# Two of a turn's 32 exponential blocks made on VectorE in the second attention

## The chip, the cores and the metric

The kernel runs on one core of a Trainium2 chip, as one program. The metric is device time in microseconds (us). Before the change it took 2643.88 us, the median of three runs (2642.66 to 2646.45). A core's engines work through instruction streams of their own and wait for each other on semaphores: TensorE (PE, matrix products into PSUM; PEld is its weight loading), ScalarE (ACT), VectorE (DVE), GpSimd (POOL) and SyncE (SP), the last two mainly issuing transfers here.

## The reference

Four layers with residuals: attention, a state-space convolution, the same attention again, the same convolution again. The change concerns the third layer, which is computed as the first one.

```python
def _A_ref(x, wqkv, wo):                     # x: 1 x 2048 x 640, 32 heads of 20
    qkv = (x @ wqkv) ... q, k, v             # by head
    scores = einsum("bhqd,bhkd->bhqk", q, k) * (Dh ** -0.5)
    p = softmax(scores, axis=-1)
    o = einsum("bhqk,bhkd->bhqd", p, v)
    return o.transpose(0, 2, 1, 3).reshape(B, S, D) @ wo

x = x + _A_ref(layernorm(x), A_wqkv, A_wo)
x = x + _B_ref(layernorm(x), ...)            # state-space convolution
x = x + _A_ref(layernorm(x), A_wqkv, A_wo)   # the second attention
x = x + _B_ref(layernorm(x), ...)
```

## The kernel before, in words

An attention goes in 32 **turns**. A turn is four heads (a group `g` of eight) and 512 of the 2048 queries. It walks over 16 tiles of 128 keys (`kt`), and for each over two pairs of heads (`j`), so it has 32 **score blocks** of 128 x 1024. For each block `scores` (L868) issues eight small products on TensorE, which fill different parts of the array together, into the PSUM tile `S`, and one exponential on ScalarE, `pt<-S`, into SBUF. There are two `S` tiles (four PSUM banks) and seven `pt` tiles (`PB`). After the two blocks of a key tile, `values` (L903) multiplies both `pt` with the values `V` into the two accumulators `pa` (one bank each, and one pair for all turns). `V` has a column of ones, so the sums of the softmax come with it. At the end of a turn VectorE copies and adds the two `pa` into `oc`; the sums of the rows go through DRAM and back by GpSimd transfers (`dn`, `dr`, `db`), VectorE inverts them, and `oc` is scaled and stored (`ot`).

Beside this TensorE has other work, in the two remaining PSUM banks `m0` and `m1`: the projections of later heads (`jobs`: `qk`, L620, 15 steps into both banks, then five VectorE operations on 128 x 512 that empty them and split the result into `qhi` and `qlo`; `vq`, L586, values of a later group; `norms`, L548), and in the last eight turns the first part of the output projection (`rows_out`, L1078, weights `woh` and `wol`, rows `oh` and `ol`). The last eight turns take the last two groups alternately.

**What sets the order.** Instructions of an engine start in the order of its program. While the program is written, a `Plan` keeps a rough clock of TensorE, ScalarE and VectorE, and it decides where things are put. After each score block `fill` runs: it issues a value product when its exponentials will be ready, then `slot` puts in steps of the projections that end before ScalarE needs a next score (`until`), and `drain_later` and `weave` put in work of VectorE whose time has come. `slot` without a limit puts the next step in whatever it delays. `chain` ties TensorE's products in the order written, and the other engines are tied likewise in an attention. Line 78 of the profile is the wrapper through which ScalarE, VectorE, GpSimd and SyncE operations are recorded.

Of the kernel before, what the change touches and what calls it, by code (L numbers as in the profile page):

```python
# [21 lines left out]
P = 128  # L22
# [20 lines left out]
MAGIC = 1.5 * 2.0 ** 23  # L43
TWO_PI = 6.283185
# [6 lines left out]
class Plan:  # L51


    def __init__(self):
        self.pe = self.act = self.dve = 0.0
        self.keep, self.fixed = False, 0.07
# [6 lines left out]
class Ordered:  # L63
# [5 lines left out]
    def __getattr__(self, name):  # L69
# [4 lines left out]
        def call(out, *a, **k):  # L74
            if self.count:
                big = a[0].shape if "reduce" in name else out.shape
                self.plan.dve = max(self.plan.dve, self.plan.pe - 0.9) + self.plan.fixed + math.prod(big[1:]) / 960
            made = f(out, *a, **k)  # L78
# [9 lines left out]
def mha_s4d_kernel(ctx, tc, x_in, wqkv, wo, lar, aim, cr, ci, ldt, dsk,  # L88
# [319 lines left out]
    pend, slow = [], []  # L408
    free = [0.0, 0.0]
# [22 lines left out]
    def attention(x, stats):  # L432
# [282 lines left out]
        def slot(until=None):  # L715
# [3 lines left out]
            begun = head[0] and head[0][2]  # L719
            if pend and part[0] is None and not begun and (head[0] is None or spent[0] >= ahead(len(ends) - 2)):  # L720
# [134 lines left out]
        plan.keep, plan.fixed = True, 0.11 if first_layer else 0.07  # L855
# [3 lines left out]
        ready, scaled, stored = [], [], {}  # L859

        def scores(kt_, kc, qt):
# [3 lines left out]
            for t in range(4):  # L865
                for r in range(2):
                    rows = slice(64 * r, 64 * r + NK)
                    chain(te.matmul(S[32 * t:32 * t + 32, 512 * r:512 * r + 512],  # L868
                                    kt_[rows, kc + 32 * t:kc + 32 * t + 32], qt[rows, :],
                                    start=True, stop=True, tile_position=(64 * r, 32 * t)))  # L870
# [24 lines left out]
        def values(qb, g, kt, pts, pa):  # L895

            V = Vt[g // 2 % 3]
            plan.on_pe(0.865)
            for r in range(2):
                rows = slice(64 * r, 64 * r + 64)  # L900
                for j in range(4):
# [3 lines left out]
                                    start=(kt == 0), stop=(kt == NI - 1), tile_position=(64 * r, 32 * j)))  # L905
            if kt == NI - 1:
# [47 lines left out]

        def end_jobs():
# [17 lines left out]
            if not first_layer:  # L973
                xpools.pop().__exit__(None, None, None)
# [18 lines left out]
        class Rows:  # L993

            def __init__(self, w2, n):
                self.w2, self.n, self.loaded = w2, n, []
                self.mv = w2.tile([P, NI, 2], F32, bufs=1, name="mvx")
                self.whole = set()
# [24 lines left out]
        def normalise(rows, x, s):  # L1023
# [18 lines left out]
            def parts():  # L1042
                u = rows.w2.tile([P, D], F32, bufs=1, name="u")
                ve.tensor_scalar(u, x[:, s, :], mv[:, 0:1], y, ALU.subtract, ALU.mult)
                ve.tensor_copy(uh[:, s, :], u)
                later.append((plan.dve + 0.5, lambda: ve.tensor_sub(ul[:, s, :], u, uh[:, s, :])))
# [47 lines left out]
        last[0] = None  # L1094
        tail, rows, stop = None, None, []
# [5 lines left out]
        for n, (g, qb) in enumerate(turns):  # L1101
# [15 lines left out]
            g2, qb2 = turns[n + 1] if n + 1 < len(turns) else (g, 0)  # L1117
            for kt in range(NI):
                kc, pts = P * (kt % 8), []
                for j in range(2):  # L1120
                    pts.append(scores(kop[j][kt // 8], kc, qop[j][n % 2]))
                    if j:
                        ready.append((plan.act, qb, g, kt, pts, pa))
                    fill(j)
# [6 lines left out]
                if kt == 12 and first_layer and n == len(turns) - 1:  # L1131
                    late.append(ve.last)
                if kt == 8 and g2 != g:
# [6 lines left out]
        for r_ in ready:  # L1140
            values(*r_[1:])
# [652 lines left out]
```

## Time and profile before

| what | us |
|---|---|
| runs: median (lowest to highest) | 2643.88 (2642.66 to 2646.45) |
| the profiled execution, first to last instruction (its span; no other time of it is given) | 2647.0 |
| second attention's score blocks, first exponential to the last | 1469 to 2451 |
| a turn there, 982 us over 32 | 30.7 |
| ScalarE busy in these 982 us | 967 |
| VectorE busy in these 982 us | 296 |

A busy TensorE in the table of the profile is not TensorE at its peak, since its ends are modelled and its products overlap. Start times in a timeline are the better measure of what it holds.

### The profile page before, as it was taken

To read this page: it belongs to the slowest core of one execution; us is meant where nothing else is said; L and a number is where in the kernel's file an instruction comes from. 1 tells how busy PE (TensorE), PEld (TensorE's weight loads), DVE (VectorE), ACT (ScalarE), POOL (GpSimd) and SP (SyncE) were. 2 spreads that over 40 slices of the span, in tenths; PEclk is the share of its full clock that TensorE was granted. 3 is DMA by queue.
4 is the path that set the end of the run, shared out by engine and by line. 5 is a ranking of instruction groups with operands and counts; after the bars stand their busy time and mean duration, and the time that the engine had idled before them with its cause. 6 is when DMAs were issued, how large, how long until landed. Compare 5 with 4: busy or idle time off the path is not lost.

```text
span 2647.0 us, 118800 instructions
## 1 busy us (share of the span) xinstructions
PE 2492.4 (94%) x52388; PEld 1409.8 (53%) x52388; DVE 1519.5 (57%) x3430; ACT 2344.0 (89%) x2763; POOL 801.7 (30%) x1230
## 2 busy tenths in 40 slices
PE   6899999999999999899898999999999998999898
PEld 3444444454444444587896544454444443444898
DVE  7587777777765887577786323232232222143875
ACT  7899999999999999655665899999999999999574
POOL 1123333233323332111681122222222223222285
PEclk9999999999999999999999999999999999999999
DMA  6522222322222221654652111121121113222466
GB/s 206 189 53 77 68 74 62 82 65 63 61 54 59 53 63 38 234 206 163 213 173 64 47 53 50 51 60 45 45 66 39 50 34 87 71 66 61 137 190 184
DMA packets 188158, 241.99 MB, mean 91 GB/s; under 512 B 43504, under 2 KB 128816, under 8 KB 186224
## 3 DMA queue, kind: packets, MB, share of 16 engines
q1 hardware_dynamic: 151936, 188.28, 22.6%
q0 software_dynamic: 35696, 46.01, 7.4%
q8 instruction: 413, 6.77, 1.1%
q14 instruction: 113, 0.93, 0.1%
HBM read 158.16 MB, written 76.00 MB: 88 GB/s over the span
## 4 chain that ended last, share of the span: by engine, by line
ACT 59%; PE 20%; issue 10%; DVE 3%; DMA 2%; POOL 1%; SPq 0%; ACTq 0%; POOLq 0%; DVEq 0%
ACT pt L78 57%; PE psy L1430 3%; PE pa L903 2%; PE psv L1430 2%; PE po L193 2%; PE psx L1430 2%; PE S L868 2%; PE pst L1452 1%; PE pkx L193 1%; PE pv L586 1%; PE m L620 1%; PE pkt L196 1%; PE pq L773 1%; DMA kb<-khb 1%; DMA kop<-ks 1%
## 5 line engine op out<-in xcount | busy, mean ns | idle before, releaser
L78 ACT ACTIVATE pt<-S 128x1024 f32<-128x1024 f32 x2048 | 1927.7, 1033 | 27.9 <-PE S L868 15.5
L903 PE MATMUL pa<-pt,V 64*32 64x512 f32 x16384 | 1096.9, 589 | 1.4 <-DVE oc L78 1.4
L868 PE MATMUL S<-qop,kop 61*32 61x512 f16 x16384 | 877.2, 380 | 82.7 <-ACT pt L78 67.8
L868 PEld LDWEIGHTS <-kop 61*32 61x32 f16 x16384 | 366.9, 89 | 737.3 <-issue 619.2
L903 PEld LDWEIGHTS pa<-pt,V 64*32 64x32 f32 x16384 | 312.7, 106 | 72.0 <-issue 8.6
L78 POOL DMA_DIRECT2D dn<-oc x248 | 122.7, 501 | 574.2 <-DVE oc L78 574.1
L78 DVE TENSOR_SCALAR qc<-m 128x512 f32<-128x512 f32 (+1 forms) x68 | 46.8, 688 | 312.0 <-PE m L620 312.0
L78 POOL DMA_DIRECT2D db<-dn x248 | 125.4, 512 | 141.5 <-DMA dn<-dr 136.9
L78 POOL DMA_DIRECT2D ot<-oc x256 | 130.5, 517 | 88.4 <-DVE oc L78 55.5
L620 PE MATMUL m<-xl,wh 64*32 64x512 f16 x2560 | 143.8, 376 | 0.3 <-issue 0.3
L620 PE MATMUL m<-xh,wh 64*32 64x512 f16 x2560 | 144.1, 378 | 0.0
L620 PE MATMUL m<-xh,wl 64*32 64x512 f16 x2560 | 143.8, 377 | 0.0
L78 DVE COPY oc<-pa 128x512 f32<-128x512 f32 x64 | 44.2, 690 | 172.9 <-PE pa L903 168.9
L78 ACT COPY xt<-pst 128x1024 f16<-128x1024 f16 x80 | 81.3, 1016 | 60.8 <-PE pst L1452 60.8
L620 PEld LDWEIGHTS <-wh 64*32 64x32 f16 x5120 | 90.3, 93 | 73.3 <-issue 30.8
L78 POOL DMA_DIRECT2D dn<-dr x62 | 34.6, 558 | 287.3 <-DVE dr L78 248.6
L1480 POOL TENSOR_TENSOR kb<-t,kb 128x512 f32<-128x512 f32 x76 | 97.2, 1280 | 65.2 <-DVE t L78 40.8
L78 DVE TENSOR_SCALAR V<-m 128x160 f32<-128x160 f32 x64 | 20.7, 324 | 163.4 <-PE m L586 163.4
L78 DVE TENSOR_TENSOR kb<-ktab 128x512 f32<-128x512 f32 x160 | 106.2, 683 | 0.0
L586 PEld LDWEIGHTS <-xh 128*128 128x128 f16 x960 | 79.7, 98 | 46.7 <-issue 31.4
L1480 POOL TENSOR_TENSOR ka<-ka,kb 128x512 f32<-128x512 f32 x76 | 97.5, 1283 | 6.0
L337 PEld LDWEIGHTS m<-kb,ka 128*32 128x32 f32 x3840 | 60.8, 109 | 71.0 <-issue 52.4
(312 smaller groups left out, 3936.4 us busy)
## 6 DMA issues: line engine op xcount, KB each, us to landing
ka<-kha SPq DMA_DIRECT2D x80, 256.0 KB
kb<-khb SPq DMA_DIRECT2D x80, 256.0 KB
db<-dn POOLq DMA_DIRECT2D x248, 64.0 KB, 3.2
kop<-ks SPq DMA_DIRECT2D x176, 80.0 KB
kpw<-wd POOLq DMA_DIRECT2D x60, 192.0 KB, 3.9
qop<-qs SPq DMA_DIRECT2D x256, 40.0 KB
ot<-oc POOLq DMA_DIRECT2D x256, 40.0 KB, 3.0
kha<-kn SPq DMA_DIRECT2D x20, 512.0 KB
```

The costliest lines, as they stand in the source:

```text
L78: made = f(out, *a, **k)
L193: chain(te.matmul(*a, **k))
L196: chain(te.transpose(*a, **k))
L337: chain(te.matmul(ps[32 * j:32 * j + 32, c8, :], a[n][:, ch, :], b[n][:, dd, :], start=(n == 0), stop=(n == 2), tile_position=(0, 32 * j)))
L586: chain(te.matmul(ps[:, :n], a_[:, ct, sl], m[:, ct, :], start=(k == 0), stop=(k == 14)))
L620: chain(te.matmul(ps[r][32 * t:32 * t + 32, :], a_[rows, ct, 32 * u:32 * u + 32], m[rows, ct, 512 * v:512 * v + 512], start=(k == 0), stop ...
L773: te.matmul(pq, a_[:, ct, :], m[:, ct, sl], start=(n == 0), stop=(n == 14))
L868: chain(te.matmul(S[32 * t:32 * t + 32, 512 * r:512 * r + 512], kt_[rows, kc + 32 * t:kc + 32 * t + 32], qt[rows, :], start=True, stop=Tru ...
L903: chain(te.matmul(pa[r][32 * j:32 * j + 32, :], V[rows, kt, VP * h:VP * h + 32], pts[j // 2][rows, 512 * (j % 2):512 * (j % 2) + 512], sta ...
L1430: at("pe", te.matmul(*a, **k))
L1452: at("pe", te.transpose(pt[:, k, g, :], of_group(x1[k], 4 * q + g), id16))
L1480: at("pool", getattr(ge, f)(*a))
```

## The change

In the second attention alone, two of a turn's 32 score blocks no longer go to ScalarE: those of the second pair of heads (`j` = 1) at key tiles 6 and 13 (`BY_DVE`; the first number of each pair is the block at which it is put on the list). Their scores are multiplied into the projections' banks `m0` and `m1`, when these are free between two units of the projections (`asked`, in `slot`). VectorE then makes an approximation of the exponential in eight operations: two read the scores out of the banks as scaled integer bits (`xbits`), two split these into mantissa (`xg`) and exponent, and four evaluate a polynomial and multiply (`xp`). The generator `exponentials` issues them one at a time, from `exps` in `fill`. In the last eight turns, when the pool `xe` is gone, tiles of `V` that are no longer used serve as buffers.

A value product is now tied to its turn (`Turn`): it is issued when both of its blocks are there, in the order in which they get ready, so key tiles 6 and 13 can come late, and those of the next turn wait until the turn is complete (`open_[0]`). Where more than two products are ready and the oldest turn has none, `fill` issues a step of VectorE and a `slot` without a limit, until it has. At `kt` 8 and at the last one, blocks that are still on the list are served in the same way. The planner's fixed cost of a VectorE operation in the second attention rises from 0.07 to 0.11, and a part of the last normalisation (`rows.rest`) is kept apart.

```diff
+LEAD = 0.01353417
+XA = SCALE * math.log2(math.e) * 2.0 ** 23
+XB = (127.0 + math.log2(LEAD)) * 2.0 ** 23
+XQ = ((2.044112790886901, 2.663560369601336), (-2.201138398968431, 14.146389192438297))
+BY_DVE = ((0, 6), (10, 13))
...
             begun = head[0] and head[0][2]
+            if asked and not begun and part[0] is None:
+                t = max(free)
+                if until and (t > plan.pe or plan.pe + 0.22 > until):
+                    return False
+                plan.on_pe(0.22, t)
+                asked.pop(0)()
+                return True
...
-        plan.keep, plan.fixed = True, 0.11 if first_layer else 0.07
+        plan.keep, plan.fixed = True, 0.11
...
+        def exponentials():
...
+            while True:
+                while not wanted:
+                    yield "wait"
+                turn, kt, j, operands = wanted.pop(0)
+                bits, g, p = buffers()
+                done = []
+
+                def begin():
+                    ps = [pst("M", [P, 512], F32, tag=f"m{r}", name=f"m{r}") for r in range(2)]
+                    products(ps, *operands)
+                    emptied(*(lambda r=r: step(ve.tensor_scalar, 0.69, bits.bitcast(mybir.dt.int32)[:, 512 * r:512 * r + 512], ps[r], XA, XB, ALU.mult, ALU.add)
+                              for r in range(2)))
+                    done.append(True)
+                asked.append(begin)
+                while not done:
+                    yield "wait"
+                bits_i = bits.bitcast(mybir.dt.int32)
+                step(ve.tensor_scalar, 0.69, g.bitcast(mybir.dt.int32), bits_i, 0x7FFFFF, 0x3F800000, ALU.bitwise_and, ALU.bitwise_or)
+                yield
+                step(ve.tensor_single_scalar, 0.69, bits_i, bits_i, 0x7F800000, ALU.bitwise_and)
+                yield
+                (a, c_), (b, d) = XQ
+                for args in ((p, g, a, g), (g, g, b, g), (p, p, c_, bits), (p, g, d, p)):
+                    step(ve.scalar_tensor_tensor, 1.224, *args, ALU.add, ALU.mult)
+                    if args[2] != d:
+                        yield
+                turn.add(kt, j, p, plan.dve)
+                yield
...
         def fill(j):
 
-            if ready:
-                t = max(ready[0][0] + 0.15, 0.0 if ready[0][3] else sums_[0])
-                if t <= plan.pe + 0.1 or j and len(ready) > 2:
+            many = sum(len(t.ready) for t in open_)
+            while many > 2 and not open_[0].ready:
+                exps(1)
+                slot()
+            if open_ and open_[0].ready:
+                turn = open_[0]
+                t = max(turn.ready[0][0] + 0.15, 0.0 if turn.issued else sums_[0])
+                if t <= plan.pe + 0.1 or j and many > 2:
                     plan.on_pe(0.0, t)
-                    values(*ready.pop(0)[1:])
+                    values(turn, *turn.ready.pop(0)[1:])
             while slot(plan.act - 0.5):
                 pass
             drain_later()
             weave()
+            exps()
...
+                if kt in (8, NI - 1):
+                    while any(w[0] is turn and (w[1] < 8 or kt > 8) for w in wanted) or asked:
+                        exps(1)
+                        if asked:
+                            slot()
```

How the instructions move shows in the order in which they now stand. First **VectorE** in the fourth and fifth turn of the second attention. Before, from the fourth turn's sum of the accumulators (`oc`) over the inverted sums (`dr`), one unit of the projections (`qc` to `qlo`) and a copy of values (`V`) to the fifth turn's `oc`:

```order
2373 L78 COPY oc<-pa_34649 128x512
2374 L78 TENSOR_TENSOR oc<-oc,pa_34650 128x512
2375 L78 TENSOR_TENSOR oc<-oc,db 128x512
2376 L78 TENSOR_SCALAR dr<-dr 128x16
2377 L78 RECIPROCAL dr<-dr 128x16
2378 L78 TENSOR_SCALAR qc<-m_35491 128x512
2379 L78 SCALAR_TENSOR_TENSOR qc<-m_35492,qc 128x512
2380 L78 TENSOR_TENSOR sq<-qc 128x512
2381 L78 CAST qhi<-qc 128x512
2382 L78 TENSOR_TENSOR qlo<-qc,qhi 128x512
2383 L78 TENSOR_SCALAR V_31425<-m_35902 128x8x20
2384 L78 COPY oc<-pa_35411 128x512
```

Now, from the end of a unit of the projections to the fourth turn's `oc`:

```order
2432 L84 CAST qhi<-qc 128x512
2433 L84 TENSOR_TENSOR qlo<-qc,qhi 128x512
2434 L84 TENSOR_SCALAR xbits<-m_35601 128x512
2435 L84 TENSOR_SCALAR xbits<-m_35602 128x512
2436 L84 TENSOR_SCALAR xg<-xbits 128x1024
2437 L84 TENSOR_SCALAR xbits<-xbits 128x1024
2438 L84 SCALAR_TENSOR_TENSOR xp<-xg 128x1024
2439 L84 SCALAR_TENSOR_TENSOR xg<-xg 128x1024
2440 L84 TENSOR_SCALAR V_31425<-m_35689 128x8x20
2441 L84 SCALAR_TENSOR_TENSOR xp<-xp,xbits 128x1024
2442 L84 SCALAR_TENSOR_TENSOR xp<-xg,xp 128x1024
2443 L84 COPY oc<-pa_34739 128x512
```

The eight operations of key tile 13 stand between the unit of the projections and the turn's `oc`; 64 such eights are added in all. `m_` and a number is a tile in the banks `m0` and `m1`. Then **TensorE** at the last score block of the third turn (`S` of the next turn begins at the end). Names in `wl` are steps of a projection, and products with `kop` are scores:

```order
35403 L627 MATMUL m_34561<-xh,wl 32x512
35404 L627 LDWEIGHTS wl
35405 L627 MATMUL m_34562<-xh,wl 32x512
35406 L881 LDWEIGHTS kop_31438
35407 L881 MATMUL m_34727<-qop_31441,kop_31438 32x512 [waits DVE_49]
35408 L881 LDWEIGHTS kop_31438
35409 L881 MATMUL m_34728<-qop_31441,kop_31438 32x512 [waits DVE_49]
```

The scores for VectorE come right behind the last step of a unit, in the same two banks, and wait for VectorE; the next turn's first score comes behind them. Last, **TensorE** at the end of the same turn's value products. Before:

```order
35405 L868 LDWEIGHTS kop_31437
35406 L868 MATMUL S<-qop_31442,kop_31437 32x512
35407 L903 MATMUL pa_33877<-pt,V_31424 32x512 x4
35408 L903 MATMUL pa_33878<-pt,V_31424 32x512 x4
35409 L868 LDWEIGHTS kop_31435
35410 L868 MATMUL S<-qop_31440,kop_31435 32x512 [waits Activation_49]
```

and now, six score blocks into the fourth turn:

```order
35623 L627 MATMUL m_34873<-xl,wh 32x512
35624 L992 MATMUL pa_33898<-pt,V_31424 32x512 x2
35625 L992 MATMUL pa_33898<-xp,V_31424 32x512 [waits DVE_49]
35626 L992 MATMUL pa_33898<-xp,V_31424 32x512
35627 L992 MATMUL pa_33899<-pt,V_31424 32x512 x2
35628 L992 MATMUL pa_33899<-xp,V_31424 32x512 x2
35629 L881 LDWEIGHTS kop_31435
35630 L881 MATMUL S<-qop_31440,kop_31435 32x512 [waits Activation_49]
```

The product that closes the turn, with `xp` of key tile 13, waits for VectorE, and the seventh score block of the next turn stands behind it. ScalarE's row of exponentials in the second attention goes from 1024 to 960.

More of the change, by code (lines that the diff above doesn't have):

```diff
@@ L55, in __init__ @@
         self.pe = self.act = self.dve = 0.0
[L56 removed]
+        self.keep, self.fixed, self.cost = False, 0.07, None
     def on_pe(self, cost, after=0.0):
@@ L861, in scores, with exps @@
+        wanted = []
+        xgen = None if first_layer else exponentials()
+        def exps(n=0):
+            while xgen and (n > 0 or plan.dve < plan.pe + 0.2):
+                if next(xgen) == "wait":
+                    break
+                n -= n > 0 and (1 if n > 1 else n + 1)
         def scores(kt_, kc, qt):
@@ L864, in scores @@
             pt = pp.tile([P, 1024], F32, name="pt")
[L865 to L870, printed above, removed]
+            products([S[:, 512 * r:512 * r + 512] for r in range(2)], kt_, kc, qt)
             se.activation(pt, S, AF.Exp, scale=SCALE)
@@ L1042, in parts @@
             def parts():
+                while rows.rest:
+                    rows.rest.pop()()
                 u = rows.w2.tile([P, D], F32, bufs=1, name="u")
@@ L1139, in attention @@
                 tail = end_jobs()
-        for r_ in ready:
-            values(*r_[1:])
+        while open_:
+            turn = open_[0]
+            while not turn.ready:
+                exps(1)
+                if asked:
+                    slot()
+            values(turn, *turn.ready.pop(0)[1:])
         if not first_layer:
```

84 lines of the change are left out of this document (72 added, 12 removed).

## The prediction

> **What bounds the kernel now.** I read the page for the shares, then the second attention by window, by groups and by waits, then timelines of a few microseconds.
>
> ```profile
> span 2647.0 us, 118800 instructions
> ACT pt L78 57%; PE psy L1430 3%; PE pa L903 2%; PE psv L1430 2%; PE po L193 2%; PE psx L1430 2%; PE S L868 2%; PE pst L1452 1%; PE pkx L193 1%; PE pv L586 1%; PE m L620 1%; PE pkt L196 1%; PE pq L773 1%; DMA kb<-khb 1%; DMA kop<-ks 1%
> ```
>
> ```profile
> 1469.00:2451.00 982.00, 941.18 (x21196) 449.55 (x21189) 295.79 (x652) 967.13 (x1025) 232.29 (x456) 1.00 0.20 55
> ```
>
> ```profile
> L78 ACT ACTIVATE pt<-S 128x1024 f32<-128x1024 f32 x1024 | 966.8, 1032 | 18.1 <-PE S L868 9.2
> ```
>
> ```profile
> PE S L868 <- ACT pt L78: 30.0, 86, 0.9
> ```
>
> The exponentials (`pt`) hold 57% of the chain of work that ended last. In the second attention (columns PE, PEld, DVE, ACT, POOL) ScalarE is busy 967 of 982 us and idle 18 us before its 1024 exponentials: 982/1024 = 0.959 us each. TensorE's scores waited for ScalarE 86 times, so TensorE has slack, but little. How little shows in a timeline:
>
> ```profile
> 2212.61 0.41 PE L868 MATMUL S<-qop,kop 61*32 61x512 f16 x8 [0.34 <-ACT pt L78]
> 2212.82 1.05 PE L903 MATMUL pa<-pt,V 64*32 64x512 f32 x16
> 2213.68 0.41 PE L868 MATMUL S<-qop,kop 61*32 61x512 f16 x8
> 2214.44 0.41 PE L868 MATMUL S<-qop,kop 61*32 61x512 f16 x8 [0.35 <-ACT pt L78]
> ```
>
> By starts, a score holds TensorE 0.21 to 0.22 us, a value product 0.86 us, and two exponentials set a pace of 1.83 us, 0.915 each, when nothing is late. With two score tiles ScalarE can't be fed far ahead:
>
> ```profile
> 1469.26 2.86 ACT L78 ACTIVATE pt<-S 128x1024 f32<-128x1024 f32 x3 [4.35 <-PE S L868]
> 1470.34 0.62 PE L868 MATMUL S<-qop,kop 61*32 61x512 f16 x8 [0.85 <-ACT pt L78]
> 1472.38 0.70 PE L868 MATMUL S<-qop,kop 61*32 61x512 f16 x8
> 1473.13 1.02 ACT L78 ACTIVATE pt<-S 128x1024 f32<-128x1024 f32 x1 [1.01 <-PE S L868]
> 1474.17 0.41 PE L868 MATMUL S<-qop,kop 61*32 61x512 f16 x8
> 1474.65 3.88 ACT L78 ACTIVATE pt<-S 128x1024 f32<-128x1024 f32 x4 [0.50 <-PE S L868]
> ```
>
> The exponential from 1469.26 lasts 1.03, and the score that reuses its tile starts 0.05 later, at 1470.34. An exponential starts 0.48 after its score (1474.17 to 1474.65). So TensorE may go 3 x 0.915 - 1.08 - 0.48 = 1.18 us from one score to the next before ScalarE starves; what is longer is lost. Here 2.04 us went by (1470.34 to 1472.38, with projections between) and ScalarE stood 1.01.
>
> **The gain.** 64 exponentials leave ScalarE: 64 x 0.915 = 59 us at most.
>
> **What VectorE takes for a block.** The nearest rows (mean ns last):
>
> ```profile
> L78 DVE TENSOR_SCALAR qc<-m 128x512 f32<-128x512 f32 x26 | 17.9, 689 | 161.7 <-PE m L620 161.7
> L78 DVE SCALAR_TENSOR_TENSOR wl<-ws,wh 128x640 f16<-128x640 f32 x6 | 5.0, 825 | 0.2
> L78 DVE SCALAR_TENSOR_TENSOR vl<-ws,vh 128x800 f16<-128x800 f32 x3 | 3.0, 993 | 0.1
> L78 DVE TENSOR_SCALAR kc__1107<-ks__1106 128x640 int32<-128x640 int32 x1 | 0.5, 494 | 0.0
> ```
>
> Reading a bank is 0.69. A two-operand operation grows by 168 ns over 160 columns, so 1.23 us at 1024. The bit operations at 1024 are not in the trace: between 0.49 (640 columns) and 1.23 (as the slow kind); its 0.494 at 640 is far from the slow kind's 0.825, and at half that kind's 1.05 ns a column it grows by 384 x 0.525 ns to 0.7, which I take. Sum: 2 x 0.69 + 2 x 0.69 + 4 x 1.23 = 7.7 us (8.7 at the upper bound). With one foreign operation between (0.3) and the hand-overs to and from TensorE (0.2) it is 8.2 us from the end of the scores to the product that needs them. 64 x 7.7 = 490 us beside VectorE's 296: 790 us of the second attention, no bound on average.
>
> **Where TensorE puts it.** I counted the new order, with the durations above. Before, no stretch between two scores passes 1.18 us but the very last. After, 81 do, together 176 us, so 176 - 81 x 1.18 = 80 us starve ScalarE, without any wait. Three places repeat each turn: block 16 (`V`, `X`, where X are the scores for VectorE), block 29 (`V`, up to nine steps of a projection, X), and block 5 of the next turn. There is worse in two waits.
>
> First, in 14 turns the X of key tile 13 stands directly behind the last step of a unit, whose banks VectorE must empty:
>
> ```profile
> 1604.42 0.41 PE L620 MATMUL m<-xh,wh 64*32 64x512 f16 x8
> 1604.85 0.41 PE L868 MATMUL S<-qop,kop 61*32 61x512 f16 x8
> 1606.15 0.41 PE L620 MATMUL m<-xh,wl 64*32 64x512 f16 x8
> 1606.79 0.63 DVE L78 TENSOR_SCALAR qc<-m 128x512 f32<-128x512 f32 x1
> 1607.52 0.69 DVE L78 SCALAR_TENSOR_TENSOR qc<-m,qc 128x512 f32<-128x512 f32 x1
> 1608.25 0.69 DVE L78 TENSOR_TENSOR sq<-qc 128x512 bf16<-128x512 f32 x1
> 1608.86 0.42 DVE L78 CAST qhi<-qc 128x512 f16<-128x512 f32 x1
> 1609.31 0.69 DVE L78 TENSOR_TENSOR qlo<-qc,qhi 128x512 f16<-128x512 f32 x1
> ```
>
> A step is 0.22 us (two from 1604.42 to 1604.85). The banks are empty some 1.65 us after the last step (1606.4 to 1608.2, a little less without the `dr` ahead); before, other scores and products filled that time. The score behind X waits too. And `sq`, `qhi`, `qlo` are ahead of X's reads on VectorE: 1.5 us more to the product.
>
> Second, this product. Its X is at block 29, and the order has it only six score blocks on, behind block 5 of the next turn; key tile 6 has 11 to 17 blocks' room. Six blocks keep ScalarE busy 5.5 us of the 8.2. The seventh pt tile is then taken as well. So TensorE stands at the product, with the next score queued behind it. The turn is a chain:
>
> - X to the product 8.2; the product 0.86; its next score to the exponential 0.48;
> - blocks 6 to 29: 23 x 0.915 = 21.05, and 0.83 for five products caught up (score and product 1.08, not 0.915, five times); block 16 0.12 (1.30 over 1.18);
> - back to the score of block 29, -0.75 (0.48 and 1.08 against two paces), then score, product, X: 0.22 + 0.86 + 0.22.
>
> That is 32.1 us, against 982/32 = 30.7. With projections (14 turns) 1.5 for VectorE's leftovers, 1.65 for the banks, 1.14 for the steps ahead of X (5.3 on average) and 0.4 at block 16 come to it: 36.8. The 24th turn issues all that is left of the projections (7.7 us without a score): 40. There all products are drained, so the 25th overlaps nothing with the 8.2: 8.2 and 1.7 for two products, 0.48, 29 x 0.915, -0.75 and 1.3, together 37.4. In turns 29 to 31 the order gives VectorE 34 to 40 us of work, since the normalisation is there already now:
>
> ```profile
> 2350.00:2400.00 50.00, 47.99 (x884) 21.55 (x871) 33.58 (x118) 48.82 (x52) 11.67 (x23) 1.00 0.23 67
> ```
>
> 33.6 of 50 us is 20.6 a turn, and 15.4 come to it: VectorE bounds these at some 36.5. Sum: 14 x 36.8 + 13 x 32.1 + 40 + 37.4 + 3 x 36.5 = 1119 us, 137 more than 982.
>
> **The tail.** 54 products of the output projection more than before (276, not 222) are in the attention, where the stretches counted hold them. The rest runs at TensorE's pace:
>
> ```profile
> 2453.00:2492.00 39.00, 39.00 (x274) 38.08 (x275) 36.73 (x109) 17.17 (x28) 11.63 (x13) 1.00 0.41 125
> ```
>
> 39 us for 274 products (0.142 each), so 54 fewer save 8. The normalisation's part kept apart moves one VectorE operation a row: no cost, up to 1 us. The planner's 0.07 to 0.11 only moves work, and is in the count. First attention and both convolutions stay.
>
> 2647.0 + 137 - 8 = 2776 us for the profiled execution; the runs' median is 2643.9 to its span of 2647.0, 3 less, so **2773 us**.
>
> [...] The softmax's sums go out by GpSimd, and VectorE now works more beside it:
>
> ```profile
> L78 POOL DMA_DIRECT2D dn<-oc x120 | 59.7, 504 | 185.5 <-DVE oc L78 185.5
> L78 POOL DMA_DIRECT2D dn<-oc x124 | 61.0, 499 | 385.4 <-DVE oc L78 385.3
> 200.00:250.00 50.00, 49.25 (x1388) 24.73 (x1379) 37.22 (x84) 49.89 (x55) 17.35 (x30) 1.00 0.32 87
> ```
>
> An issue takes 504 ns in the first attention (150 to 1050 us), where VectorE is busy 37 of 50 us, and 499 in the second (1500 to 2450) at 15 of 50. [...]
>
> **Rivals.**
> - *The product finds its operand ready* (VectorE ahead, or its chain short). Then only the stretches cost: -59 + 80 - 8 = +13, with the banks' waits (14 x 1.65 = 23) +36: 2657 to 2680. For it: VectorE has slack. Against it: 8.2 us don't fit in 5.5. Chance 0.16.
> - *VectorE's lateness spreads.* Each emptying of a bank or of `pa` can stand behind a 1.23 us operation, 0.6 on average, six a turn, in the 18 turns with over 25 us of VectorE: +65, 2838. For it: VectorE issues in order; against: the planner knows these costs. Chance 0.12.
> - *ScalarE stays fed, and it gets faster.* A turn below 30.7 needs X to product in 8.2 - 1.4 = 6.8 us, and no waits for banks. That is so if the four long operations ran at the bit operations' rate, 0.7 (chain 6.1), and VectorE came to the banks during the steps. Then a turn is 30 x 0.959 = 28.8, so 32 x 28.8 - 982 - 8 = -69: 2575. Against it: the rows at 640 and 800 columns, and the order. Chance 0.08.
> - [...] Chance 0.04.
> - *No difference*, gain and starving even: 0.02. That it doesn't do what it says is out: ScalarE's row in the order has 960, not 1024.
>
> **How the numbers follow.** The forecast has 0.58; its own bounds are 2725 (chain 1.5 us shorter a turn, if VectorE's operations overlap) to 2820 (bit operations at 1.23: 1 us a turn, and half as much for waits between units). 8 in 10 takes in most of the first rival and half of the second: 2660 to 2850. A change under 0.2%, about 5 us, can't be told from none here. Slower has 0.58 + 0.16 + 0.12 + 0.04 = 0.90, faster 0.08, same 0.02.
>
> **What would show it.** Right: 960 exponentials at an unchanged mean; ScalarE idle before `pt` 150 to 250 us, released by TensorE's scores; TensorE's value products waiting for VectorE's `xp` about once a turn, 3 to 5 us; X waiting for `qc`; VectorE 770 to 800 us busy there; long operations at 1.23. Wrong: an attention near 30.7 us a turn or below, value products without waits for VectorE, or ScalarE idle under 50 us.

## The result, and the profile after

The changed kernel takes 2900.56 us (median of four runs, 2898.4 to 2903.54), the kernel before 2644.03 beside it: a ratio of 1.0967, 95% interval 1.0951 to 1.0982. That is 256.5 us slower, where 129 were forecast. From the page of the changed kernel, the span and the chain of work that ended last:

```profile
span 2901.7 us, 119130 instructions
...
ACT pt L84 38%; PE pa L992 9%; PE S L881 5%; PE m L627 3%; DVE xp L84 3%; PE psy L1561 2%; DVE V L84 2%; PE psv L1561 2%; PE po L199 2%; PE psx L1561 2%; DVE xg L84 1%; DVE qc L84 1%; PE pst L1583 1%; DVE xbits L84 1%; PE pkx L199 1%
```

ScalarE's exponentials no longer hold 57% of the chain but 38%; value products (`pa`) have 9 and not 2, and VectorE's `xp`, `V`, `xg`, `qc` and `xbits` are on it now.

The window of the second attention (busy us of PE, PEld, DVE, ACT, POOL; then the granted clock) and its groups (count, busy us, mean ns, then the engine's idle us ahead of them and what ended it):

```profile
1470.00:2698.00 1228.00, 1058.74 (x21230) 485.62 (x21236) 764.04 (x1213) 915.18 (x962) 235.48 (x456) 0.96 0.16 44
```

```profile
L84 ACT ACTIVATE pt<-S 128x1024 f32<-128x1024 f32 x960 | 915.0, 1031 | 316.9 <-PE S L881 261.9 <-PE pa L992 46.0
...
L84 DVE TENSOR_SCALAR xbits<-m 128x512 int32<-128x512 f32 x96 | 61.6, 683 | 30.9 <-PE m L881 30.9
...
L84 DVE SCALAR_TENSOR_TENSOR xp<-xg,xp 128x1024 f32<-128x1024 f32 x48 | 58.7, 1224 | 1.5
...
L84 DVE TENSOR_SCALAR xbits<-xbits 128x1024 int32<-128x1024 int32 x48 | 34.7, 723 | 1.5
L84 DVE TENSOR_SCALAR xg<-xbits 128x1024 int32<-128x1024 int32 x48 | 31.8, 663 | 0.7
```

The attention is 1228 us and not 982, with 52 us less of exponentials in it; ScalarE is idle for 316.9 us ahead of them and was for 18.1. (VectorE's rows count 48 of the 64 blocks; those of the last eight turns have tiles of `V` as buffers and stand under that name.) What TensorE and ScalarE waited for there (us in total, times, longest):

```profile
ACT pt L84 <- PE S L881: 261.9, 78, 14.2
...
PEld pa L992 <- DVE xp L84: 71.4, 24, 6.0
...
PE S L881 <- ACT pt L84: 53.2, 116, 0.9
PE pa L992 <- DVE xp L84: 47.7, 24, 5.1
ACT pt L84 <- PE pa L992: 46.0, 30, 2.3
...
PE m L881 <- DVE qc L84: 24.6, 42, 0.8
```

TensorE's weight loads stood 71.4 us in all before 24 products that need `xp`, once a turn in the first 24 turns: 3.0 us each. The row of the products (47.7) shows the same 24 waits once more, from the end of the product before; the two are not to be added. A timeline from the end of the third turn shows how:

```profile
1585.17 0.40 PE L627 MATMUL m<-xh,wl 64*32 64x512 f16 x8
1585.64 0.69 DVE L84 TENSOR_SCALAR qc<-m 128x512 f32<-128x512 f32 x1 [2.13 <-PE m L627]
...
1587.18 0.41 PE L881 MATMUL m<-qop,kop 61*32 61x512 f16 x7 [0.42 <-DVE qc L84]
...
1587.95 5.93 ACT L84 ACTIVATE pt<-S 128x1024 f32<-128x1024 f32 x6 [3.93 <-PE S L881]
...
1596.05 0.32 DVE L84 TENSOR_SCALAR V<-m 128x160 f32<-128x160 f32 x1
1596.29 1.22 DVE L84 SCALAR_TENSOR_TENSOR xp<-xp,xbits 128x1024 f32<-128x1024 f32 x1
1596.42 0.41 PE L627 MATMUL m<-xh,wh 64*32 64x512 f16 x7 [1.97 <-DVE V L84]
...
1597.54 1.23 DVE L84 SCALAR_TENSOR_TENSOR xp<-xg,xp 128x1024 f32<-128x1024 f32 x1
1598.82 1.07 PE L992 MATMUL pa<-xp,V 64*32 64x512 f32 x2 [0.45 <-DVE xp L84]
...
1600.78 0.69 DVE L84 COPY oc<-pa 128x512 f32<-128x512 f32 x1 [2.02 <-PE pa L992]
1601.25 1.02 ACT L84 ACTIVATE pt<-S 128x1024 f32<-128x1024 f32 x1 [7.37 <-PE S L881]
...
1604.34 1.94 ACT L84 ACTIVATE pt<-S 128x1024 f32<-128x1024 f32 x2 [2.06 <-PE pa L992]
```

X waits for the banks (its first product starts at 1586.38, the rest at 1587.18), and the next score stands behind it: ScalarE has stood 3.93 us when its next exponential starts, at 1587.95. Six exponentials are done at 1593.88. TensorE meanwhile waits for a `V` that stands in VectorE's order between X's operations, then for `xp`; the product starts 11.2 us after the end of X (1587.18 + 0.41), and ScalarE starves for 7.37. Then it stands once more, 2.06 us, since no `pt` tile is free.

For the comparison of kernels, the starts of the exponentials from 1460 us on: 0.907 us is about the distance when nothing is late, and what is beyond it is added up by the score block at which it falls (31 turns; the 24th apart). These sums, in us, carry most of what follows:

| kernel | all | block 5 | block 6 | 16, 17 | block 29 | 24th turn | other blocks |
|---|---|---|---|---|---|---|---|
| before | 53 | 6.5 | 1.5 | 4.2 | 2.4 | 0.7 | 37.5 |
| changed | 358 | 156.5 | 48.3 | 31.0 | 55.6 | 30.8 | 35.7 |
| result unread | 323 | 68.5 | 99.9 | 31.1 | 55.6 | 19.5 | 48.6 |
| same, six operations left out | 241 | 52.0 | 47.3 | 31.8 | 55.5 | 19.5 | 34.9 |
| order only | 193 | 57.5 | 46.7 | 16.5 | 21.7 | 15.3 | 35.6 |
| prompt product | 174 | 3.7 | 4.4 | 41.8 | 55.3 | 29.5 | 39.1 |

(Blocks are counted from 0; with two of them on VectorE a turn has blocks 0 to 29 on ScalarE.) Four places and one turn hold the whole difference of 305 us; against it stand 64 x 0.907 = 58 us of exponentials that are gone.

### The profile page after: what moved, and what is told of

Its sections match the earlier page's. It is cut to its first block, busy times and chain, and to the rows that moved or that the text cites. A ratio compares the mean times of both kernels' runs of the same rounds, so it can differ in the third digit from the quotient of the medians.

```text
span 2901.7 us, 119130 instructions
## 1 busy us (share of the span) xinstructions
PE 2607.0 (90%) x52388; PEld 1438.4 (50%) x52388; DVE 1985.8 (68%) x3960; ACT 2288.1 (79%) x2694; POOL 802.3 (28%) x1229
## 4 chain that ended last, share of the span: by engine, by line
ACT 40%; PE 32%; DVE 13%; issue 8%; DMA 1%; POOL 1%; SPq 0%; ACTq 0%; DVEq 0%; POOLq 0%
ACT pt L84 38%; PE pa L992 9%; PE S L881 5%; PE m L627 3%; DVE xp L84 3%; PE psy L1561 2%; DVE V L84 2%; PE psv L1561 2%; PE po L199 2%; PE psx L1561 2%; DVE xg L84 1%; DVE qc L84 1%; PE pst L1583 1%; DVE xbits L84 1%; PE pkx L199 1%
## 5 line engine op out<-in xcount | busy, mean ns | idle before, releaser
L84 ACT ACTIVATE pt<-S 128x1024 f32<-128x1024 f32 x1984 | 1875.6, 1032 | 327.8 <-PE S L881 269.5
L992 PE MATMUL pa<-pt,V 64*32 64x512 f32 x15872 | 1176.0, 597 | 3.3 <-DVE oc L84 3.3
L881 PE MATMUL S<-qop,kop 61*32 61x512 f16 x15872 | 896.9, 385 | 108.7 <-ACT pt L84 91.1
L992 PEld LDWEIGHTS pa<-pt,V 64*32 64x32 f32 x15872 | 329.2, 107 | 113.4 <-DVE oc L84 24.4
L627 PE MATMUL m<-xh,wh 64*32 64x512 f16 x2560 | 153.4, 386 | 4.5 <-DVE V L84 3.8
L84 POOL DMA_DIRECT2D dn<-dr x62 | 34.9, 562 | 438.1 <-DVE dr L84 379.9
L627 PE MATMUL m<-xh,wl 64*32 64x512 f16 x2560 | 153.4, 387 | 0.0
L627 PE MATMUL m<-xl,wh 64*32 64x512 f16 x2560 | 150.1, 382 | 0.0
L627 PEld LDWEIGHTS <-wh 64*32 64x32 f16 x5120 | 92.2, 94 | 88.6 <-issue 48.3
L84 DVE TENSOR_SCALAR V<-m 128x160 f32<-128x160 f32 (+1 forms) x96 | 41.2, 443 | 128.7 <-PE m L593 91.9
L84 DVE COPY oc<-pa 128x512 f32<-128x512 f32 x64 | 44.2, 690 | 86.5 <-PE pa L992 85.4
L992 PE MATMUL pa<-xp,V 64*32 64x512 f32 x384 | 59.3, 689 | 47.7 <-DVE xp L84 47.7
```

Of the source, the lines that this page charges most:

```text
L627: chain(te.matmul(ps[r][32 * t:32 * t + 32, :], a_[rows, ct, 32 * u:32 * u + 32], m[rows, ct, 512 * v:512 * v + 512], start=(k == 0), stop ...
L881: chain(te.matmul(outs[r][32 * t:32 * t + 32, :], kt_[rows, kc + 32 * t:kc + 32 * t + 32], qt[rows, :], start=True, stop=True, tile_positi ...
L992: chain(te.matmul(pa[r][32 * j:32 * j + 32, :], V[rows, kt, VP * h:VP * h + 32], pts[j // 2][rows, 512 * (j % 2):512 * (j % 2) + 512], sta ...
```

## The experiments

The theory at first was: the product of key tile 13 stands too close behind its scores; TensorE's wait, the half clock after it and the late release of `pt` tiles are most of the loss. The rivals: VectorE's load makes everything late that passes through it, or the rest of the change costs time without any block.

**No block on VectorE.** The rest of the change stays.

```diff
-BY_DVE = ((0, 6), (10, 13))
+BY_DVE = ()
```

> No block goes to VectorE (the list is empty), all 1024 exponentials are ScalarE's; the rest of the change stays: value products in the order in which they get ready, the planner's cost, the normalisation's part kept apart. If VectorE's blocks are the whole loss: no difference from before, 2638 to 2650 us. If the new order itself loses time: 2700 us or more.

Measured: 2648.17 us, ratio 1.0009 (1.0000 to 1.0019). The planner's cost, the products' free order and the part kept apart cost nothing that can be told. All of the loss comes with the blocks.

**The result unread.** The operations stay; the product takes ScalarE's tile of that key tile twice.

```diff
-                turn.add(kt, j, p, plan.dve)
+                turn.add(kt, j, None, plan.dve)
...
+                    pts = [v or pts[1 - n] for n, v in enumerate(pts)]
```

> Everything as in the change, VectorE's eight operations of each block too, but the value product reads ScalarE's exponential of the same key tile twice and not VectorE's result (which nobody reads): no product waits for VectorE. Theory (the product stands too close behind its scores; its wait, the half clock after the wait and the late release of pt tiles are most of the loss): 2670 to 2730 us, exponentials' gap at block 5 and block 6 gone, and fewer than 5 spells of half clock in the second attention. Rival (VectorE's load makes everything late that goes through VectorE): 2820 us or more.

Measured: 2863.8 us, 1.0837 (1.0814 to 1.0860), only 37 us less. The theory in this form fell. The waits of this kernel tell why:

```profile
ACT pt L84 <- PE S L881: 171.4, 92, 12.4
...
ACT pt L84 <- PE pa L993: 98.1, 30, 6.6
PEld pa L993 <- DVE oc L84: 77.0, 60, 5.1
...
PE pa L993 <- DVE oc L84: 48.6, 29, 4.7
```

In place of `xp`, TensorE now waits for `oc`, the copy of the accumulators at the turn's end, which VectorE has behind X's operations in its order: 77.0 us by its weight loads (20.7 in the changed kernel); the products' 48.6 are mostly the same time again. Block 5 lost 88 us less and block 6 52 more. Whatever is taken from VectorE there comes late, not one operand.

**The six operations left out as well.** The reading of the banks stays, and the order everywhere else (`skip` only advances the planner's clock).

```diff
-                step(ve.tensor_scalar, 0.69, g.bitcast(...
+                skip(ve.tensor_scalar, 0.69, g.bitcast(...
...                                       # the other five likewise
```

> As the run with the unread result, and VectorE's six operations on SBUF of each block are left out as well; the two that empty the banks stay, and the order on the other engines is the same. Theory: 0 to 20 us less than the run with the unread result, since VectorE's load by itself costs little. Rival (load): at least 80 us less than that run.

Measured: 2778.4 us, 1.0508 (1.0491 to 1.0526): 85 us less than the run with the unread result, as the rival said. But 133 us are lost still, without these six operations.

**The same two blocks, served earlier.** All of the change's work is done here.

```diff
-BY_DVE = ((0, 6), (10, 13))
+BY_DVE = ((0, 6), (8, 13))
...
-                while not wanted:
+                while not wanted or not xe and any(t.g < NG - 2 for t in open_):
...
-                if kt in (8, NI - 1):
-                    while any(w[0] is turn and (w[1] < 8 or kt > 8) for w in wanted) or asked:
+                if kt in (4, 10):
+                    while any(w[0] is turn and (w[1] < 8 or kt > 4) for w in wanted) or asked:
```

> The change's own work in full, two blocks of each turn on VectorE, but their scores are put into the banks at score blocks 9 and 20 and not at 16 and 29, so 9 to 18 score blocks lie between scores and product (6 in the change for key tile 13). Theory: no product waits for VectorE; what is left are stretches of TensorE's order (53 beyond 1.18 us, 63 us too long in all, 16 of it where the projections end) and some 20 bank waits of 1.65: 2660 to 2720 us. Rival (load): 2820 us or more, since VectorE has the same work.

Measured: 2757.69 us, 1.0419 (1.0401 to 1.0436). Products hardly wait for `xp` now (three times, 1.3 us in all), and with VectorE's whole work this kernel is 143 us faster than the changed one, and 21 faster than that without the six operations. So VectorE's load as such isn't the cause: it costs where TensorE wants something from VectorE a few blocks later. Still 113 us are lost, more than the theory said: 59.7 at block 20, where X again follows a unit's last step, 25 at blocks 8 to 10, and 34.8 in the 24th turn.

**The order only.** X, the reading of the banks and the six operations are left out; the order of everything else is the change's.

```diff
-                    ps = [pst("M", [P, 512], F32, tag=f"m{r}", name=f"m{r}") for r in range(2)]
-                    products(ps, *operands)
+                    ps = [None, None]
...                                       # emptied() and the six operations with skip, the product as above
```

> The order of the change on every engine, but VectorE's blocks are left out altogether: neither their scores in the banks, nor the reading of the banks, nor the six operations; the value product reads ScalarE's exponential of the key tile twice. What is left over the kernel before is the order alone (960 exponentials, TensorE's long stretches, products six blocks late). Theory: the scores in the banks with their waits (42 waits of 0.8 us for the emptying of the banks in the profile of after, and the starts behind them) are 25 to 45 us, so 2730 to 2755. Rival (the banks' waits cost nothing, the order does it all): 2765 to 2785, as with the reads.

Measured: 2726.92 us, 1.0309 (1.0291 to 1.0327). Putting X into the banks and reading it out costs 51 us, then, a little more than the theory said: blocks 29 and 16 lose 49 us less without it. The order alone, with VectorE and the banks out of play, costs 82 us.

**The product at once.** As the run without the six operations, but the product is put into the order as soon as X is.

```diff
                     done.append(True)
+                    turn.add(kt, j, None, plan.act)
...
-                turn.add(kt, j, p, plan.dve)
```

> As the run that has the scores and the reading of the banks but not the six operations, with the product issued as soon as its scores are, so that no product of a turn waits behind six score blocks of the next one. Theory: the lateness of the products in the order (projection steps put in while VectorE works, products caught up, and all seven pt tiles taken) is what block 5 and block 6 lose there, 99 us in that profile: 2665 to 2705. Rival (these losses have another cause and move with the order): 2750 us or more.

Measured: 2717.26 us, 1.0265 (1.0249 to 1.0281). Blocks 5 and 6 go from 99 us to 8, which the theory said; 10 more are lost at block 16 and 10 in the 24th turn, and the tail is 9 us longer, so 61 of the 99 are left as gain, and the time is 12 us above the theory's range. The late place of the product in the order costs this even when its operand is there: steps of the projections are put in while the product isn't due, and then no `pt` tile is free. In the order-only run, where VectorE does nothing for the blocks, the wait for a tile is the same as in the change, and all of it falls at block 6:

```profile
ACT pt L84 <- PE S L881: 98.4, 65, 10.0
...
ACT pt L84 <- PE pa L995: 44.1, 30, 2.5
```

**The clock kept up.** In the first 24 turns three more products (repeats with ScalarE's tile, so that the sums come out too large) fill TensorE's wait.

```diff
+            for _ in range(3 if kt == 13 and xe and not first else 0):
+                for r in range(2):
+                    ...
+                        chain(te.matmul(pa[r][32 * j:32 * j + 32, :], V[rows, kt, VP * (4 * (g % 2) + j):][:, :32],
+                                        pts[0][rows, 512 * (j % 2):512 * (j % 2) + 512], ...
```

> The change, with three more value products (repeats with ScalarE's exponential of that key tile, 0.86 us each at full clock) ahead of each product that needs VectorE's result of key tile 13 in the first 24 turns, where TensorE stands 5 us on average: the wait becomes work, and the sums come out too large. Theory (the granted clock falls to half because TensorE stands, 99 us at half clock in the second attention, and TensorE then lacks about half of that): at most 8 spells in place of 21, and 2845 to 2880 us. Rival (the half clock costs nothing since ScalarE sets the pace, or it has another cause): 2895 us or more.

Measured: 2893.29 us, 1.0931 (1.0911 to 1.0950). In windows of 1 us the changed kernel has 21 spells at half clock, 99 us together; this one 9, 41 us. The weight loads' waits for `xp` fell from 71.4 us to 15.6. Yet the time is only 7 us less, near the rival's figure: most of the half clock goes with the wait. How little it costs by itself isn't exactly shown, since the fill isn't free. It is 2.6 us in a turn, and the products' waits were 0.5 to 5.1, 2.0 on average (not 5, as I had taken them), so in the turns with a short wait it delays the product, by up to 19 us in all. With these the 58 us of half clock that went are worth at most some 27 us, an estimate, of the 256 lost.

**One block.** Key tile 13 alone, its scores early.

```diff
-BY_DVE = ((0, 6), (10, 13))
+BY_DVE = ((2, 13),)
```

> One block of a turn (key tile 13) on VectorE, its scores at score block 17 and its product 12 to 22 blocks later: 992 exponentials. Theory: no product waits; 32 x 0.907 = 29 us gained and about 24 us lost in three stretches without scores, where the projections have to be finished (4.9, 6.7 and 13.9 us): 2640 to 2665 us, that is, same to 0.8% slower. Rival (each block that VectorE makes costs what it did in the change, 315 us for 64 blocks without their gain): 2770 us.

Measured: 2707.16 us, 1.0222 (1.0205 to 1.0238), between the two. No product waits for `xp`, but two new losses stand in this profile:

```profile
ACT pt L84 <- PE S L881: 92.7, 35, 21.4
...
PEld L881 <- DMA kop<-ks: 28.8, 18, 4.2
...
PE m L881 <- DMA kop<-ks: 20.8, 12, 3.7
```

(The two rows with `kop` are mostly the same waits, seen at the weight loads and at the products.) The longest, 21.4 us, is in the 24th turn, where all that is left of the projections is issued in one piece; and X, early now, needs keys whose transfer (`kop`) hasn't landed. The next runs part these two.

**TensorE relieved.** Two thirds of the steps in a unit of the projections of query and key are left out (the products with the low halves), without a block and with one.

```diff
-                            for a_, m in ((w[0], xh), (w[0], xl), (w[1], xh)):
+                            for a_, m in ((w[0], xh), (w[0], xl), (w[1], xh))[:3 if first_layer else 1]:
...
```

> No block on VectorE, and TensorE relieved: a unit of the projections of query and key in the second attention has 5 steps and not 15 (the products with the low halves of weights and rows are left out). That is 69 us less for TensorE, some 45 us of which the order fills with output projection that then is missing from the tail. ScalarE still has 1024 exponentials, so the attention should stay within 10 us of 980 us, and the whole comes to 2590 to 2610 by the shorter tail.

> The same relief of TensorE, and one block of a turn (key tile 13) on VectorE as in the run with one block; 998 exponentials, since the last turns come out with fewer. Theory (the gain of 0.9 us a turn is lost where TensorE has no room and the projections come due): with room the attention is 10 to 25 us shorter than in the relieved run without VectorE, and the tail about 9 longer, so the whole is 0 to 20 us faster than that run. Rival (a VectorE block costs more than it brings with TensorE's room or without): 40 us or more slower than that run, as without the relief.

Measured: 2650.33 us without a block, 1.0014 (1.0005 to 1.0024), and 2659.3 with one, 1.0041 (1.0026 to 1.0056). The relief alone brings nothing: from the first exponential's start to the last one's it has 990 us, where the kernel before has 980, and why wasn't settled. My expectation of a shorter tail was wrong: 186 products of the output projection moved into the attention (136 of each of the three kinds, not 74) and the tail, the time after the last exponential, fell by 7 us only, 197.2 to 189.9. With the block, both theory and rival missed: 48 us of the 63 lost with one block are gone, but it is 9 us slower than the relieved run without. The waits for `kop` are still there:

```profile
PEld L881 <- DMA kop<-ks: 31.3, 18, 4.8
PE m L881 <- DMA kop<-ks: 23.4, 12, 4.4
```

**Key tile 6 in place of 13**, relieved and not. Its keys are in the half that is loaded a turn earlier, and the weight loads' waits for `kop` fall to 4.4 us relieved and 1.9 not. The generator's wait for `open_` of the run served early is in both.

```diff
-BY_DVE = ((2, 13),)
+BY_DVE = ((0, 6),)
```

> The same relief of TensorE and one block of a turn on VectorE, but key tile 6 in place of 13. In the relieved run with key tile 13 the block's scores come before the second half of the group's keys is loaded: TensorE waits there 21.5 us for the transfer of kop, at the first turn of four groups (5.4 to 7.3 us each between two exponentials). Key tile 6 is in the first half, which was loaded a turn before. Theory (only this wait hid the gain, TensorE has room): the waits for kop are gone, the attention is 970 to 980 us, and the whole 2625 to 2645: faster than the relieved run without VectorE (2650) by 5 to 25 us. Rival (the block costs more than it brings): 2650 us or more.

> One block of a turn on VectorE, key tile 6, without any relief of TensorE: 992 exponentials. Theory (the waits for kop of key tile 13 go, some 50 us less than the run with one block, but the projections still come due: stretches of 3.9, 6.5, 3.5 and 17.9 us without a score): 2650 to 2670 us. Rival (the stretches cost nothing much, kop was the whole loss): 2625 to 2640 us.

Measured: 2633.73 us relieved, 0.9957 (0.9941 to 0.9974), the only run below the kernel before, and 16.6 below the relieved run without a block (some 14 when each is taken against the kernel before beside it); 2684.23 not relieved, 1.0141 (1.0126 to 1.0157), where theory and rival both were lower. (It is 23 us less than with key tile 13, not the 50 of the expectation, which adds the two rows with `kop`.) The relieved result is in the theory's range, but it leaves out work that the kernel before does. The pages' rows of the exponentials (the first attention's 1024 are in them), first relieved without a block, then relieved with key tile 6, then that one not relieved:

```profile
L84 ACT ACTIVATE pt<-S 128x1024 f32<-128x1024 f32 x2048 | 1930.1, 1033 | 37.8 <-PE S L881 24.2
```

```profile
L84 ACT ACTIVATE pt<-S 128x1024 f32<-128x1024 f32 x2022 | 1908.1, 1033 | 38.9 <-PE S L881 23.0
```

```profile
L84 ACT ACTIVATE pt<-S 128x1024 f32<-128x1024 f32 x2016 | 1901.0, 1033 | 85.9 <-PE S L881 69.5
```

With room on TensorE, 26 exponentials fewer are 22 us less and ScalarE stands no longer than without them. Without the room it stands 47 us more, and most of that is one place, in the 24th turn:

```profile
2194.80 1.03 ACT L84 ACTIVATE pt<-S 128x1024 f32<-128x1024 f32 x1
2224.44 1.03 ACT L84 ACTIVATE pt<-S 128x1024 f32<-128x1024 f32 x1 [28.61 <-PE S L881]
```

| us | TensorE as it is | relieved |
|---|---|---|
| no block | 2648.2 | 2650.3 |
| key tile 13 | 2707.2 | 2659.3 |
| key tile 6 | 2684.2 | 2633.7 |

Key tile 13 costs some 24 us over 6 in both columns (the generator's wait for `open_` is in the lower row alone, so the difference holds its effect too), and the missing room some 50 with either; without a block the room is worth nothing. In a turn ScalarE's time is also the time in which TensorE does the projections; a block less is 0.9 us less of it, and the projections stay as long. They come due unfinished.

**Half the load.** First in the last eight turns alone (one block, key tile 13), then key tile 6 in every other turn of the first 24 and in the last eight. The line shown is the second's; the first has `not (g >= NG - 2)` in its place.

```diff
-            by_dve = () if first_layer or not xe and g < NG - 2 else BY_DVE
+            by_dve = () if first_layer or not xe and g < NG - 2 or not (n % 2 or g >= NG - 2) else BY_DVE
```

> One block of a turn on VectorE in the last eight turns only (1016 exponentials), where no projections of heads are due. Theory (TensorE sets the end: what ScalarE gains in the attention, 8 x 0.9 = 7 us, is output projection that goes into the tail): 2640 to 2650 us, no difference. Rival (ScalarE sets the end): 2635 us.

> As the run with key tile 6, in every other turn of the first 24 and in the last eight: 1004 exponentials; one stretch of 9.9 us is left where the projections end. Theory (TensorE has no room, what ScalarE gains is given back): 20 x 0.907 = 18 us gained, some 12 lost in stretches, up to 10 in the last eight turns and the tail: 2640 to 2652 us, no difference that can be told. Rival: 2630 us.

Measured: 2657.8 us, 1.0040 (1.0027 to 1.0054), and 2656.18, 1.0037 (1.0023 to 1.0050). Both are some 10 us slower than before, where no difference was expected. The attention of the second run takes 981 us from the first exponential's start to the last one's, 980 before: 18 us of exponentials gained, 15 of them lost in one gap of the 24th turn. The tail after the last exponential is 205 us in both, and was 197. In part that is output projection left to it: 298 and 308 products come after the last exponential here, 268 in the kernel before. But the run without a block has 276 and a tail of 203, and the five kernels that have the change's order in the last turns all leave 204 and take from 194 to 207 us. What else makes it vary wasn't settled. No version that computes the whole beat the kernel before.

## Why the prediction was wrong

The direction held, and the waits that were named came; but the largest loss beyond the forecast is at a place for which the sum had no term, and 2900 lies 50 above the range.

- **What VectorE takes** was right: 2 x 0.683 + 0.663 + 0.723 and four long operations at 1.212 to 1.224 are 7.63 us, where 7.7 was said. The gain of 64 exponentials at an unchanged mean (1031 ns) was right as well.
- **"Where TensorE puts it", 80 us, is the step that failed most.** The stretches counted, less the gain and the tail, made 13 us; the order alone costs 82. The count took a late product as a matter of TensorE's time only. That the seventh `pt` tile is then taken was said, but no time was put down for it: a product that is put off holds its tiles, and ScalarE waits for one at block 6 (46.7 us in the order-only run, 1.5 before). Block 5 has 57.5 there (6.5 before), where long stretches of products and steps now stand between two scores.
- **The banks' waits, 23 us by 14 turns of 1.65, cost 51.** For key tile 13 X did wait in 14 turns, 17.2 us. But X of key tile 6 waited too, at block 16, in nine turns (7.4 us), which was not in the sum; the row's 42 waits count both banks. X itself holds TensorE for 64 x 0.22 = 14 us; how the rest of the 51 is made up isn't shown.
- **The wait for VectorE was named at its place, and too small:** 129 - 13 - 23 = 93 us in the forecast, 123 from the run without the six operations to the changed kernel. From the end of X (0.22 us after its last product's start) to the end of VectorE's last operation the shortest time was 7.75 us, as the sum said; for key tile 13 the mean of 32 turns was 9.8, where 8.2 and 9.7 were said for the two kinds of turn. What is late next was missed: the loop that waits for the product also issues steps of the projections, which wait for banks behind X's operations (the 1.97 at 1596.42), and `oc` comes behind them all, as the unread result showed.
- **The turns** were to take 32.1 (no projections) or 36.8 us, 804 for the first 23; these took 32.6 to 45.1, 872 together. The 24th, said at 40, took 58.0 (42.5 in the order-only run). The 25th was overestimated, 37.4 for 29.2. Turns 29 to 31, said at 36.5 because VectorE would bound them, took 36.8, 44.2 and 47.7; the order-only run, without VectorE's blocks, has 33.7, 40.1 and 39.6 there, so most of that is the order and not VectorE.
- **The tail** was 7 us longer (203.9 after the last exponential, 197.2 before), not 8 shorter. With the same 204 products left the order-only run has 194.0, 3 us shorter than before. That the rest runs at TensorE's pace no longer holds; the first 40 us of the tail, before and now (TensorE's busy time first, the clock third from the end):

```profile
2449.80:2489.80 40.00, 39.70 (x285) 37.58 (x282) 37.02 (x105) 16.93 (x28) 11.24 (x13) 1.00 0.41 127
```

```profile
2697.80:2737.80 40.00, 28.28 (x203) 23.75 (x200) 32.47 (x64) 11.06 (x20) 7.36 (x10) 0.83 0.37 114
```

The order-only run has a clock of 1.00 there; whether the clock makes the difference isn't shown.

- **Rivals.** That the product finds its operand ready (2657 to 2680) is out by 24 waits. "VectorE's lateness spreads" (2838) was nearest, and has a real part, the 85 us of the six operations when nobody reads their result: it should have been added to the forecast, not set beside it. The 0.04 in the sum of the chances stands for the softmax's sums held up on GpSimd by a busier VectorE; no run shows that:

```profile
L84 POOL DMA_DIRECT2D dn<-oc x100 | 48.8, 495 | 360.4 <-DVE oc L84 360.3 <-issue 0.2
```

An issue takes 495 ns with VectorE busy 764 us in the attention, and took 499 with 296; and VectorE never stands before `dr` in the changed attention, where it stood 17 times, 61.5 us, before.

- **"What would show it"**: VectorE's 764 us (770 to 800 said), value products waiting for `xp` once a turn (3.0 us by the weight loads, the longest 6.0, where 3 to 5 was said) and X waiting for `qc` came. ScalarE's idle time was outside: 316.9 us, not 150 to 250.

## What to carry to other kernels

Before work is moved from the busiest engine to an idle one, count the room of the engine that feeds both: here ScalarE's time in a turn was also TensorE's time for other work, and one block less per turn paid only after TensorE had been relieved (key tile 6: 2633.7 us against 2650.3 relieved, 2684.2 against 2648.2 not). Here a result from VectorE, which worked its queue in order (the ten numbered 2434 to 2443 in the program start in that order, 1633.73 to 1643.44), cost not its own duration (7.63 us) but everything in that queue until the consumer came (9.8 from the end of X, on average for key tile 13), and what was held meanwhile (`pt` tiles, for which ScalarE waited 46.0 us; banks, 24.6 before X; accumulators, 20.7 before the value products' weight loads); so ask for it early, but not before its inputs have landed (28.8 us of waits for `kop` with one block). When one wait is taken away and the time hardly moves (37 us of 256 with the result unread), look at what the same queue owes next.

## What was unexpected on the chip

TensorE's clock fell to half again and again: 21 spells in the attention of the changed kernel, 99 us, against one of 3.4 us before, each of 3.4 us or two or three times that. Four windows of 4 us around the wait shown above (clock: the third number from the end):

```profile
1594.00:1598.00 4.00, 2.03 (x23) 0.48 (x20) 3.93 (x5) 0.00 (x0) 0.00 (x0) 0.91 0.00 0
1598.00:1602.00 4.00, 3.55 (x47) 1.53 (x50) 1.87 (x3) 0.75 (x1) 0.00 (x0) 0.50 0.02 4
1602.00:1606.00 4.00, 3.90 (x68) 1.61 (x58) 0.87 (x2) 1.94 (x3) 3.44 (x8) 0.74 0.07 12
1606.00:1610.00 4.00, 4.00 (x112) 1.95 (x97) 0.00 (x0) 3.94 (x5) 1.06 (x3) 1.00 0.18 37
```

Products last 1.06 us there (the row at 1598.82 holds two of them); the median of those that read `xp` is 0.59. In the four microseconds in which the clock fell here (1594 to 1598) TensorE was busy for 2.03. What starts a spell and what ends it isn't shown; with the waits filled there were 9 and not 21. That run also gives a bound on the price: 58 us less at half clock came with 7 us less time, at most some 27 by the estimate above. The spells went with the loss and were a small part of its cause.
